# A comparison on GpSimd written with one operation or with two, in a fused attention and feed-forward kernel

## The chip, the cores and the metric

The kernel runs on one core of a Trainium2 chip. A core has five engines that run side by side and meet at semaphores: TensorE (PE, matrix products; its weight loads are shown apart as PEld), VectorE (DVE), ScalarE (ACT), GpSimd (POOL) and SyncE (SP, which here issues transfers). The metric is the device time of one execution in microseconds, as the median of several executions. The kernel before takes 563.74 us (563.67 to 563.99 in 3 runs).

## The reference

Eight batches of eight heads go through attention in which every score that lies more than tau = 0.02 below its row's maximum is dropped. The result, 4608 rows of 512, goes through an RMS norm and a gated feed-forward layer.

```python
scores = scale * np.matmul(q, k.transpose(0, 1, 3, 2))          # 8 x 8 x 576 x 576, head size 64
thresh = np.max(scores, axis=-1, keepdims=True) - tau
scores = np.where(scores >= thresh, scores, -1000000000.0)
attn = np.exp(scores - np.max(scores, axis=-1, keepdims=True))
attn = attn / (np.sum(attn, axis=-1, keepdims=True) + 1e-09)
x = np.matmul(attn, v)                                          # heads side by side: 4608 x 512
xn = x / np.sqrt(np.mean(x * x, axis=-1, keepdims=True) + 1e-06) * rms_g
g = xn @ w_gate                                                 # 512 -> 1536
out = (g * (1.0 / (1.0 + np.exp(-g))) * (xn @ w_val)) @ w_out   # 1536 -> 512
```

The change concerns the third line: the choice of the scores that stay.

## The kernel before

The work is cut into 144 steps. A step is 128 rows of queries and two heads (h = 0 and 1). PE writes the scores of a step to PSUM (`s_ps`). DVE copies them to SBUF (`ssb`), with the sign turned and scaled, and takes the minimum over each row on the way (`mx`), so a high score is a low number there. GpSimd adds tau to it; this is the row's threshold (`nth`):

```python
def ttr(o, h=h):                                   # L592, DVE
    nc.vector.tensor_tensor_reduce(
        out=ssb[a][:, h], in0=s_ps[h][:, ROW_AT:ROW_AT + S], in1=zrow, scale=-1.0 / 8.0, scalar=3.0e38,
        op0=ALU.add, op1=ALU.min, accum_out=mx[m][:, h:h + 1])
...
def nthr(o):                                       # L599, GpSimd
    nc.gpsimd.tensor_scalar(out=nth[m], in0=mx[m], scalar1=tau, scalar2=None, op0=ALU.add)
```

The dropping and the exponential are done in one of two ways for each head of a step. From step 16 on, head 1 of every even step goes the way "g", and all else the way "p":

```python
if way == "p":
    def prelu(o, h=h):                             # L610, ACT: scores below the threshold become hugely negative
        nc.scalar.activation(out=ssb[a][:, h], in_=ssb[a][:, h], func=PRELU, scale=-1.0,
                             bias=nth[m][:, h:h + 1], **PRELU_KW)
    def ex(o, h=h):                                # L614, ACT
        nc.scalar.activation(out=wsb[s % NW][:, h], in_=ssb[a][:, h], func=AF.Exp)
    def ex2(o):                                    # L617, ACT: both heads at once, where both go this way
        nc.scalar.activation(out=wsb[s % NW], in_=ssb[a], func=AF.Exp)
    ...
else:
    def ex(o, h=h, es=es):                         # L629, ACT
        nc.scalar.activation(out=esb[es], in_=ssb[a][:, h], func=AF.Exp, scale=-1.0,
                             bias=nth[m][:, h:h + 1])
    ...
        def mask(o, h=h):                          # L643, GpSimd: 1 where the score stays, else 0
            nc.gpsimd.tensor_scalar(
                out=wsb[s % NW][:, h], in0=ssb[a][:, h], scalar1=nth[m][:, h:h + 1], scalar2=None,
                op0=ALU.is_le)
        def take(o, h=h, es=es):                   # L648, GpSimd: times the exponential
            nc.gpsimd.tensor_tensor(out=wsb[s % NW][:, h], in0=wsb[s % NW][:, h], in1=esb[es],
                                    op=ALU.mult)
```

From step 16 on the weights `wsb` of a step are turned by a transposing DMA (`wt<-wsb`, L677, issued by SyncE). After every odd step PE multiplies the transposed weights of the two steps with V (L696, L700), and DVE divides by the row sums (L717, L718). Four steps make a chunk of 128 rows of x. For each chunk ACT sums squares, and GpSimd normalizes:

```python
def mean(o):                                       # L732, L734, GpSimd
    nc.gpsimd.tensor_scalar(out=irm[i3], in0=ssq[i3], scalar1=1.0 / DM, scalar2=1e-6,
                            op0=ALU.mult, op1=ALU.add)
    nc.gpsimd.tensor_tensor(out=ir[i3], in0=irm[i3], in1=mhalf, op=ALU.pow)
def norm(o):                                       # L737, GpSimd
    nc.gpsimd.tensor_scalar(out=xn[ci % 2], in0=xsb[ci % 2], scalar1=ir[i3], scalar2=1.0,
                            op0=ALU.mult, op1=ALU.mult)
```

GpSimd also rounds V and the weights of the feed-forward layer to float16 (L487, L937), in the same two-operation form. The feed-forward layer (L795, L800, L865 on PE; L809 on ACT; L812, L817 on DVE) runs in between, on chunks that are complete. The instructions of all engines are put into one fixed order before the program is built, by a list scheduler with a table of estimated costs; the estimates set the order only.

Of the kernel before, what the change touches and what calls it, by code (L numbers as in the profile page):

```python
# [11 lines left out]
ALU = mybir.AluOpType  # L12
# [115 lines left out]
def kernel(  # L128
# [26 lines left out]
    def sb(name, shape, dt=FP32):  # L155
        return konst.tile(shape, dt, tag=name, name=name)
# [26 lines left out]
    ssb = [sb(f"ssb{i}", [128, 2, S]) for i in range(NSS)]  # L183
    NES = 3
    mx = [sb(f"mx{i}", [128, 2]) for i in range(6)]
    nth = [sb(f"nth{i}", [128, 2]) for i in range(6)]
    esb = [sb(f"esb{i}", [128, S], FP16) for i in range(NES)]
    NW = 3
    wsb = [sb(f"wsb{i}", [128, 2, S], FP16) for i in range(NW)]
# [31 lines left out]
    def add(eng, cost, prio, deps, fn, **kw):  # L221
        o = Op(eng, cost, prio, deps, fn, **kw)
        ops.append(o)
        return o
# [361 lines left out]
    def emit_softmax(s, so):  # L586

        a = s % NSS
        m = s % 6
        for h in range(2):  # L590
            def ttr(o, h=h):
# [4 lines that stand above are left out]
            ttr_of[s, h] = add("DVE", COST["ttr"], s - 1, [so, o_c] + exp_of.get(s - NSS, []), ttr)  # L596

        def nthr(o):
            nc.gpsimd.tensor_scalar(out=nth[m], in0=mx[m], scalar1=tau, scalar2=None, op0=ALU.add)  # L599

        tn = add("POOL", COST["pool_tiny"], s - 4, [ttr_of[s, 0], ttr_of[s, 1]], nthr)
        wfree = [w_read.get(s - NW)]
        done = []
        ways = WAYS[s % len(WAYS)] if s >= FIRST else "pp"
        pls = []
        for h in range(2):
            way = ways[h]
            if way == "p":
                def prelu(o, h=h):
                    nc.scalar.activation(out=ssb[a][:, h], in_=ssb[a][:, h], func=PRELU, scale=-1.0,  # L610
                                         bias=nth[m][:, h:h + 1], **PRELU_KW)

                def ex(o, h=h):
                    nc.scalar.activation(out=wsb[s % NW][:, h], in_=ssb[a][:, h], func=AF.Exp)  # L614

                def ex2(o):
                    nc.scalar.activation(out=wsb[s % NW], in_=ssb[a], func=AF.Exp)  # L617

                pls.append(add("ACT", COST["prelu"], s + 0.5, [tn], prelu))
                if ways != "pp":  # L620
                    done.append(add("ACT", COST["exp0"], s + 0.5, pls + wfree, ex))
                elif h:
                    done.append(add("ACT", COST["exp2"], s + 0.5, pls + wfree, ex2))
            else:
                es = pre.get("n", 0) % NES
                pre["n"] = pre.get("n", 0) + 1

                def ex(o, h=h, es=es):
                    nc.scalar.activation(out=esb[es], in_=ssb[a][:, h], func=AF.Exp, scale=-1.0,  # L629
                                         bias=nth[m][:, h:h + 1])  # L630

                e = add("ACT", COST["exp1"], s + 0.4, [tn, pre.get(("es", es))], ex)
                if way == "d":
                    def mask(o, h=h, es=es):
                        nc.vector.scalar_tensor_tensor(
                            out=wsb[s % NW][:, h], in0=ssb[a][:, h], scalar=nth[m][:, h:h + 1], in1=esb[es],
                            op0=ALU.is_le, op1=ALU.mult)

                    st = add("DVE", COST["mask_d"], s + 0.4, [e] + wfree, mask)
                    done.append(st)  # L640
                else:
                    def mask(o, h=h):
                        nc.gpsimd.tensor_scalar(  # L643
                            out=wsb[s % NW][:, h], in0=ssb[a][:, h], scalar1=nth[m][:, h:h + 1], scalar2=None,
                            op0=ALU.is_le)

                    def take(o, h=h, es=es):
                        nc.gpsimd.tensor_tensor(out=wsb[s % NW][:, h], in0=wsb[s % NW][:, h], in1=esb[es],  # L648
                                                op=ALU.mult)

                    mk = add("POOL", COST["mask_g"], s + 0.4, [tn] + wfree, mask)
                    st = add("POOL", COST["take_g"], s + 0.4, [e, mk], take)
                    done.append(mk)
                pre["es", es] = st
                done.append(st)
        exp_of[s] = done

        if s < N_PE or s < N_ALT and s % 2:
            def tr(o):
                for j in range(9):  # L660
                    r, c = divmod(j, 5)
                    nc.tensor.transpose(ring[o.slot[r]].bitcast(FP16)[:, 128 * c:128 * c + 128],  # L662
                                        wsb[s % NW].rearrange("p h s -> p (h s)")[:, 128 * j:128 * j + 128], id16)

            t = add("PE", COST["trw"], s + 2.4, done + av_of.get(s - NWT, []), tr, ring="R", nring=2)
            w_read[s] = t
            w_ready[s] = []
            for r, (lo, hi) in enumerate(((0, 5), (5, 9))):
                def ev(o, r=r, lo=lo, hi=hi):
                    eng = nc.gpsimd if W_EVAC[r] == "POOL" else nc.vector  # L670
                    eng.tensor_copy(out=wt[s % NWT][:, lo:hi], in_=ring[t.slot[r]].bitcast(FP16)[
                        :, 0:128 * (hi - lo)].rearrange("p (c n) -> p c n", n=128))

                w_ready[s].append(add(W_EVAC[r], COST["evac_w" if W_EVAC[r] == "DVE" else "evac_wp"], s + 2.4, [t], ev, frees=(t, r)))
        else:
            def tdma(o):
                nc.sync.dma_start_transpose(out=wt[s % NWT], in_=wsb[s % NW].rearrange("p h s -> p (h s)"))  # L677

            t = add("SP", COST["sp_tr"], s, done + av_of.get(s - NWT, []), tdma, dma=DMA_NS['wt'])
            w_read[s] = t  # L680
            w_ready[s] = [t]
# [265 lines left out]
    for j in range(4):  # L947
        o = add("POOL", COST["pool_dma"], W_FROM + W_STEP * n + j + WO_AT, [], lambda o, j=j: nc.gpsimd.dma_start(
            out=wo[:, 3 * j:3 * j + 3], in_=wo_src[:, 3 * j:3 * j + 3]), dma=DMA_NS['wo'], bulk=True)
# [111 lines left out]
```

## Time and profile before

| engine | busy, us | what it mostly does |
|---|---|---|
| PE | 554.2 | scores, products with V, feed-forward layer |
| ACT | 460.0 | exponentials, `prelu`, tanh |
| DVE | 425.3 | copy with minimum, gating, dividing |
| POOL | 322.4 | comparison 110.5, product with the exponential 81.8, thresholds 31.7, normalizing 25.0 |

The span of the profiled execution is 561.9 us, and the granted TensorE clock is full throughout. The times of engines overlap, so they don't add up to the span. In the page, a group of instructions is shown by its line in the kernel, its engine and operation, and what it writes and reads; then comes how often it ran, its busy time, the mean of one in ns, and the idle time of its engine right before it with the engine, tile and line that ended it. An engine that is busy for half the span may still hold up the others, and one that is idle costs nothing if nobody waits for it; so the chain that ended last and the waits are read beside the busy times.

### The profile page before, as it was taken

What the parts mean: (1) busy time and instruction counts of PE and PEld (TensorE: products, weight loads), DVE (VectorE), ACT (ScalarE), POOL (GpSimd) and SP (SyncE); (2) the same over time, 40 slices, a digit from 0 to 9 for tenths busy, and PEclk for the clock granted to TensorE, in tenths of its full rate; (3) what the DMA queues carried; (4) which work ended last, traced back from release to release, by engine and by line L of the source; (5) the groups of instructions that cost most, each with busy time, mean ns of one, the idle gap of its engine ahead of it and who ended that gap; (6) DMA issues with size and microseconds to landing.
All of it is one profiled execution on the core that took longest, in us unless ns stands there. A gap on an engine that the chain in (4) does not pass through costs nothing.

```text
span 561.9 us, 15217 instructions
## 1 busy us (share of the span) xinstructions
PE 554.2 (99%) x5768; PEld 316.4 (56%) x5768; DVE 425.3 (76%) x1091; ACT 460.0 (82%) x741; POOL 322.4 (57%) x462
## 2 busy tenths in 40 slices
PE   8999999999999999999999999999999999999997
PEld 4756666757667455545555455545555444445674
DVE  4989977869968589658885889578966886586354
ACT  5999999998989788879888997888988988885332
POOL 2378846975767456665667666666666664551000
PEclk9999999999999999999999999999999999999999
DMA  9999999889976499889997799989998544652211
GB/s 200 271 291 250 173 179 216 161 143 198 195 181 115 116 174 160 185 156 183 154 176 175 121 170 176 182 177 156 174 189 179 110 97 97 151 95 53 85 38 38
DMA packets 270025, 89.08 MB, mean 159 GB/s; under 512 B 252544, under 2 KB 262272, under 8 KB 269952
## 3 DMA queue, kind: packets, MB, share of 16 engines
q1 hardware_dynamic: 267168, 86.02, 76.4%
q0 software_dynamic: 1600, 1.57, 1.7%
q8 instruction: 45, 0.74, 0.6%
q10 hardware_dynamic: 1184, 0.52, 0.3%
q14 instruction: 28, 0.23, 0.1%
HBM read 37.75 MB, written 9.44 MB: 84 GB/s over the span
## 4 chain that ended last, share of the span: by engine, by line
PE 95%; DVE 2%; POOL 1%; ACT 1%; issue 1%; DVEq 0%; POOLq 0%
PE s_ps L569 29%; PE ring L795 17%; PE ring L800 16%; PE ring L865 15%; PE ring L700 6%; PE ring L304 2%; PE ring L696 2%; DVE ssb L592 1%; PE ring L662 1%; PE ring L365 1%; PE s_ps L800 1%; PE s_ps L840 1%; PE s_ps L865 1%; PE s_ps L262 1%; PE s_ps L795 0%
## 5 line engine op out<-in xcount | busy, mean ns | idle before, releaser
L592 DVE CUSTOM_DVE_ANT_0 ssb<-s_ps,zrow 128x576 f32<-128x576 f32 x288 | 207.1, 753 | 64.3 <-PE s_ps L569 46.5
L610 ACT ACTIVATE ssb<-ssb,nth 128x576 f32<-128x576 f32 x224 | 166.1, 767 | 26.7 <-POOL nth L599 26.2
L569 PE MATMUL s_ps<-qkt 64*64 64x288 f32 (+1 forms) x1792 | 166.4, 417 | 1.5 <-DVE mx L592 1.5
L643 POOL TENSOR_SCALAR wsb<-ssb,nth 128x576 f16<-128x576 f32 x64 | 110.5, 1726 | 11.6 <-DMA wt<-wsb 6.3
L795 PE MATMUL ring<-xnT,wg 128*128 128x256 f16 (+1 forms) x564 | 114.4, 325 | 0.3 <-DVE xsb L718 0.3
L569 PEld LDWEIGHTS s_ps<-qkt 64*64 64x64 f32 (+1 forms) x1792 | 78.4, 140 | 62.8 <-DVE mx L592 15.5
L800 PE MATMUL ring<-xnT,wv 128*128 128x512 f16 (+1 forms) x528 | 110.4, 331 | 0.0
L599 POOL TENSOR_SCALAR nth<-mx 128x2 f32<-128x2 f32 x144 | 31.7, 220 | 128.6 <-DVE mx L592 114.4
L812 DVE SCALAR_TENSOR_TENSOR sl<-th,ring 128x256 f32<-128x256 f32 (+1 forms) x141 | 77.0, 546 | 30.5 <-ACT th L809 29.5
L617 ACT ACTIVATE wsb<-ssb 128x1152 f16<-128x1152 f32 x80 | 93.0, 1162 | 3.4 <-DMA wt<-wsb 1.1
L809 ACT ACTIVATE th<-ring 128x256 f32<-128x256 f32 (+1 forms) x141 | 67.7, 481 | 30.7 <-PE ring L795 26.6
L865 PE MATMUL ring<-wo,hf 128*128 128x512 f16 x384 | 90.0, 380 | 0.0
L648 POOL TENSOR_TENSOR wsb<-wsb,esb 128x576 f16<-128x576 f16 x64 | 81.8, 1279 | 10.1 <-ACT esb L629 5.7
L817 DVE TENSOR_TENSOR hf<-ring,sl 128x512 f16<-128x512 f32 (+1 forms) x132 | 75.0, 568 | 9.3 <-PE ring L800 0.5
L800 PEld LDWEIGHTS <-wv 128*128 128x128 f16 x576 | 52.2, 98 | 44.5 <-issue 14.2
L795 PEld LDWEIGHTS <-wg 128*128 128x128 f16 x576 | 52.0, 98 | 42.2 <-issue 12.2
L865 PEld LDWEIGHTS <-hf 128*128 128x128 f16 x408 | 37.3, 98 | 47.0 <-issue 7.0
L629 ACT ACTIVATE esb<-ssb,nth 128x576 f16<-128x576 f32 x64 | 49.2, 769 | 6.4 <-POOL nth L599 6.0
L700 PE MATMUL ring<-va,wt 128*128 128x65 f16 (+1 forms) x1264 | 52.9, 193 | 0.0
L700 PEld LDWEIGHTS <-wt 128*128 128x128 f16 (+1 forms) x1280 | 48.7, 100 | 3.8 <-issue 0.7
L614 ACT ACTIVATE wsb<-ssb 128x576 f16<-128x576 f32 x64 | 43.6, 681 | 1.6
L696 PE MATMUL ring<-va,wt 128*128 128x130 f16 (+1 forms) x158 | 35.1, 227 | 0.6 <-ACT qTv L473 0.6
(68 smaller groups left out, 444.8 us busy)
## 6 DMA issues: line engine op xcount, KB each, us to landing
vst<-in_v_dram SPq DMA_DIRECT2D x32, 256.0 KB, 3.8
qkn<-in_k_dram SPq DMA_DIRECT2D x31, 256.0 KB, 4.5
out_dram<-osb SPq DMA_DIRECT2D x31, 256.0 KB, 2.8
qkn<-in_q_dram SPq DMA_DIRECT2D x28, 256.0 KB, 4.2
stage<-in_moe_w_gate_dram SPq DMA_DIRECT2D x6, 512.0 KB, 6.1
stage<-in_moe_w_val_dram SPq DMA_DIRECT2D x6, 512.0 KB, 6.2
wt<-wsb SPq DMA_TRANSPOSE x128, 3.2
wo<-in_moe_w_out_dram POOLq DMA_DIRECT2D x4, 384.0 KB, 6.9
```

What stands on the lines that cost most here:

```text
L569: nc.tensor.matmul(s_ps[h][rows, ROW_AT + n * part:ROW_AT + n * part + n], lhs(hs), kT[i][p][h][hs, n * part:n * part + n], start=True, st ...
L592: nc.vector.tensor_tensor_reduce(out=ssb[a][:, h], in0=s_ps[h][:, ROW_AT:ROW_AT + S], in1=zrow, scale=-1.0 / 8.0, scalar=3.0e38, op0=ALU.a ...
L610: nc.scalar.activation(out=ssb[a][:, h], in_=ssb[a][:, h], func=PRELU, scale=-1.0, bias=nth[m][:, h:h + 1], **PRELU_KW)
L617: nc.scalar.activation(out=wsb[s % NW], in_=ssb[a], func=AF.Exp)
L643: nc.gpsimd.tensor_scalar(out=wsb[s % NW][:, h], in0=ssb[a][:, h], scalar1=nth[m][:, h:h + 1], scalar2=None, op0=ALU.is_le)
L648: nc.gpsimd.tensor_tensor(out=wsb[s % NW][:, h], in0=wsb[s % NW][:, h], in1=esb[es], op=ALU.mult)
L700: nc.tensor.matmul(ring[o.slot[0]][rs, at:at + D + 1], w[:, 5 * h + j, rs], va[vi][:, p, 2 * j + h], start=False, stop=(h == 1 and j == 3))
L795: nc.tensor.matmul(ring[o.slot[0]][:, 0:n], wg[d][:, fs], xnT[slot][:, d, 0:n], start=(d == 0), stop=(d == 3))
L800: nc.tensor.matmul(ring[o.slot[0]][:, 0:n], wv[d][:, fs], xnT[slot][:, d, 0:n], start=(d == 0), stop=(d == 3))
L812: nc.vector.scalar_tensor_tensor(out=sl[i][:, 0:n], in0=th[i][:, 0:n], scalar=1.0, in1=ring[g.slot[0]][:, 0:n], op0=ALU.add, op1=ALU.mult)
L817: nc.vector.tensor_tensor(out=hf[hi][:, 0:n], in0=ring[vv.slot[0]][:, 0:n], in1=sl[i][:, 0:n], op=ALU.mult)
L865: nc.tensor.matmul(ring[(first or o).slot[0]], hf[hs[fc][0]][:, 128 * j:128 * (j + 1)], wo[:, fc], start=(fc == 0), stop=(fc == NFC - 1))
```

## The change

The comparison L643 gets a second operation, a multiplication by 1.0. The value stays 0 or 1, so the result is the same. It is meant to give GpSimd the comparison in the form that its other long operations in this kernel have. The order of instructions and the estimates of the scheduler stay as they are.

```diff
                     def mask(o, h=h):
                         nc.gpsimd.tensor_scalar(
-                            out=wsb[s % NW][:, h], in0=ssb[a][:, h], scalar1=nth[m][:, h:h + 1], scalar2=None,
-                            op0=ALU.is_le)
+                            out=wsb[s % NW][:, h], in0=ssb[a][:, h], scalar1=nth[m][:, h:h + 1], scalar2=1.0,
+                            op0=ALU.is_le, op1=ALU.mult)
```

## The prediction

> **What bounds the kernel now.** I read the page from the top: busy shares, then the slices of the span, then the chain that ended last. After that I asked the trace for the busy time by stretches, for the groups of GpSimd by form, and for the waits of PE and of GpSimd.
>
> ```profile
> PE 554.2 (99%) x5768; PEld 316.4 (56%) x5768; DVE 425.3 (76%) x1091; ACT 460.0 (82%) x741; POOL 322.4 (57%) x462
> PE   8999999999999999999999999999999999999997
> POOL 2378846975767456665667666666666664551000
> PE 95%; DVE 2%; POOL 1%; ACT 1%; issue 1%; DVEq 0%; POOLq 0%
> ```
>
> PE is busy in 99% of the span, in every slice, and makes up 95% of the chain that ended last; POOL (GpSimd), the engine that the change touches, is busy 57% and holds 1% of the chain. The changed instruction runs between 59.6 and 503.3 us only. In that stage the busy time by stretches reads:
>
> ```profile
> 60.00:500.00 440.00, 439.09 (x4675) 243.90 (x4673) 342.90 (x875) 383.34 (x613) 281.38 (x381) 1.00 0.84 161
> ```
>
> The columns are the stretch, its length, then busy time of PE, PE's weight loads, DVE, ACT and POOL. PE lacks 440.00 − 439.09 = 0.9 us of being busy throughout. GpSimd is idle for 440.00 − 281.38 = 158.6 us. PE's own list of waits names no DMA and no GpSimd:
>
> ```profile
> PE s_ps L569 <- DVE mx L592: 1.5, 4, 0.4
> PE s_ps L262 <- DVE zrow L257: 1.2, 1, 1.2
> PE ring L696 <- ACT qTv L473: 0.6, 1, 0.6
> ```
>
> So the kernel waits for TensorE's work, and a better GpSimd instruction can at most remove waits that PE hardly has.
>
> [...] So the 99% may hide short stalls; here the weight loads are busy for 56% only. I therefore allow some microseconds more than the visible 0.9. [...] The trace agrees with the reported spans here: a mask starts at 202.62 and its product at 204.43, 1.81 us apart, for a mask of 1.73 us.
>
> [...]
>
> **The change, part by part.** It takes no instruction away and adds none. 64 comparisons (one head of every even step from step 16 on) get a second operation, a multiplication by 1.0. Their output is 0 or 1 as before. Order, semaphores and buffers stay. What can change is the duration of one instruction. The groups of GpSimd by form:
>
> ```profile
> L643 POOL TENSOR_SCALAR wsb<-ssb,nth 128x576 f16<-128x576 f32 x64 | 110.5, 1726 | 11.6 <-DMA wt<-wsb 6.3
> L648 POOL TENSOR_TENSOR wsb<-wsb,esb 128x576 f16<-128x576 f16 x64 | 81.8, 1279 | 10.1 <-ACT esb L629 5.7
> L599 POOL TENSOR_SCALAR nth<-mx 128x2 f32<-128x2 f32 x144 | 31.7, 220 | 128.6 <-DVE mx L592 114.4 <-DVE rz L717 3.1 <-DMA wt<-wsb 2.8
> L737 POOL TENSOR_SCALAR xn<-xsb,ir 128x512 f16<-128x512 f32 x36 | 25.0, 695 | 3.7
> L732 POOL TENSOR_SCALAR irm<-ssq 128x1 f32<-128x1 f32 x36 | 6.9, 190 | 21.9 <-ACT xn L729 19.6
> ```
>
> The comparison (L643) has one operation; it takes 1726 ns for 576 elements a partition. Normalizing x (L737) is the same kind of instruction, float32 in and float16 out, a scalar by the row, but with two operations (multiply, multiply by 1.0): 695 ns for 512. Two lines through these points:
> - two operations: L732 with 1 element 190 ns, L737 with 512 elements 695 ns: (695 − 190) / 511 = 0.99 ns an element.
> - one operation: L599 with 2 elements 220 ns, L643 with 576 elements 1726 ns: (1726 − 220) / 574 = 2.62 ns an element.
>
> The single form is also 30 ns dearer at hardly any elements, and L599 is an addition, not a comparison. This speaks for a better loop behind the two-operation form, not only for a slow comparison. But no row shows one operation of arithmetic on a long tile, nor a comparison with two. Three outcomes for the instruction:
> - **The pair takes the better loop** (my 60%): 190 + 575 × 0.99 = 759 ns, estimated from the rows above[...]. At 759 ns GpSimd saves 64 × (1726 − 759) = 62 us, and its busy time falls from 322 to some 260 us.
> - **The comparison sets the rate** and the multiplication adds little (25%): 1.7 to 2.0 us, GpSimd +0 to +18 us.
> - **The pair falls onto a slower loop** (15%): 3 us or more, GpSimd +80 us or more.
>
> **What of it lies on the path.** GpSimd's stream in one pair of steps:
>
> ```profile
> 202.62 1.73 POOL L643 TENSOR_SCALAR wsb<-ssb,nth 128x576 f16<-128x576 f32 x1
> 204.43 1.28 POOL L648 TENSOR_TENSOR wsb<-wsb,esb 128x576 f16<-128x576 f16 x1
> 205.80 0.19 POOL L732 TENSOR_SCALAR irm<-ssq 128x1 f32<-128x1 f32 x1
> 206.07 0.57 POOL L734 TENSOR_TENSOR ir<-irm,mhalf 128x1 f32<-128x1 f32 x1
> 206.74 0.69 POOL L737 TENSOR_SCALAR xn<-xsb,ir 128x512 f16<-128x512 f32 x1
> 207.52 0.23 POOL L599 TENSOR_SCALAR nth<-mx 128x2 f32<-128x2 f32 x1
> 210.39 0.21 POOL L599 TENSOR_SCALAR nth<-mx 128x2 f32<-128x2 f32 x1 [2.65 <-DVE mx L592]
> 210.71 1.73 POOL L643 TENSOR_SCALAR wsb<-ssb,nth 128x576 f16<-128x576 f32 x1
> ```
>
> The weights of the even step are complete at 204.43 + 1.28 = 205.71; their transposing DMA is issued at 205.74 and, with the page's median of 3.2 us to landing, is there at 208.9. The product with V that needs them (L696) starts on PE at 216.38, together with the odd step's weights, which are issued at 210.44 and there at 213.6. A mask 0.97 us shorter brings the even weights sooner to a consumer that leaves them lying 7.4 us already. The odd step's threshold at 207.52 could come sooner too, as DVE's maximum was ready at about 206.3; but the product with V has 216.38 − 213.6 = 2.8 us to spare there. And right after, GpSimd waits 2.65 us for DVE. So most of the saved 62 us turns into waits for DVE's maximum, which are 114.4 us already. ACT's waits for the threshold, 26.2 us (L610) and 6.0 us (L629), may shrink, but ACT at 82% doesn't bound either.
>
> Contention: the maximum on DVE (L592) takes 746 to 759 ns over all its 288 runs, with the mask beside it or not. [...] I count nothing for it.
>
> The sum with the better loop: −0.9 us at most from visible PE idle time in the stage, of which a part is due to other things, and as much again from hidden stalls: −0.5 us as the middle, −2.5 at best. With the comparison setting the rate: 0 to +0.5 us.
>
> **Rivals.** (1) GpSimd becomes the bound. Against it: 158.6 us idle in the stage over 64 masks is 2.5 us for each, so a mask must grow to about 4.2 us before GpSimd is full. But its stream is in order, and thresholds sit behind masks, so from about 3.5 us PE would wait: at 4.5 us I'd expect (4.5 − 4.2) × 64 = 19 us and some more for waits, 3 to 6% slower. This needs the slower loop, and a bad one. (2) The transposing DMAs are the real gate, and weights that come sooner move them into other loads. For it: the DMA engines are 84% busy in the stage, and one pair of transposes took 3.96 us to issue. Against it: PE names no wait for a DMA. It would make ±1 us. (3) PE's 99% hides stalls that GpSimd causes through the chain threshold, ACT, weights. For it: weight loads waited 17.4 us for DVE's maximum. Against it: those gaps are about 0.4 us, as long as gaps with no releaser, and GpSimd is not named. If a third of it went, the time would be 558 us, still within 2%.
>
> **Range and chances.** 0.60 × (−0.5) + 0.25 × (+0.2) leaves about −0.3; the slow loop is a tail, not the middle. I say 563.2 us. The range from 560.5 to 566.0 us holds the first two outcomes and a mild form of the third. 2% is 11.3 us: faster by that would need stalls that no view shows (2%); slower needs a mask above some 4 us (8%).
>
> **What would show it.** [...] PE's busy time at 552 to 555 us, its waits as before. The step fails if the mask stays near 1.7 us. The conclusion fails if PE's busy time or idle time moves by more than 3 us, or if waits of PE for transposed weights appear.

## The result, and the profile after

The changed kernel takes 568.5 us (568.31 to 568.87 in 4 runs) against 563.87 us before (563.67 to 564.53 in 4 runs): a ratio of 1.0079, with a 95% interval from 1.0065 to 1.0093. It is 4.6 us slower, outside the predicted range of 560.5 to 566.0 us, though within 2%. The order of the instructions is the same on every engine.

First the groups of GpSimd by form, as shown of before (busy us, mean ns, then the idle time in front and what ended it):

```profile
L643 POOL TENSOR_SCALAR wsb<-ssb,nth 128x576 f16<-128x576 f32 x64 | 142.0, 2219 | 8.4 <-DMA wt<-wsb 3.0
L648 POOL TENSOR_TENSOR wsb<-wsb,esb 128x576 f16<-128x576 f16 x64 | 81.8, 1278 | 9.7 <-ACT esb L629 5.2
L599 POOL TENSOR_SCALAR nth<-mx 128x2 f32<-128x2 f32 x144 | 31.9, 221 | 107.6 <-DVE mx L592 86.8 <-DVE rz L717 7.0 <-DMA wt<-wsb 5.1
```

The comparison went from 1726 to 2219 ns. That is 0.49 us more for each of 64, or 31.6 us of GpSimd. Its neighbours didn't move. Then the busy times, and the shares of the chain that ended last:

```profile
PE 557.7 (98%) x5768; PEld 318.3 (56%) x5768; DVE 425.1 (75%) x1091; ACT 458.1 (81%) x741; POOL 354.1 (63%) x462
PE 91%; DVE 3%; ACT 2%; issue 2%; DMA 1%; POOL 1%; SPq 0%; DVEq 0%; ACTq 0%; POOLq 0%
```

GpSimd has 31.7 us more and still idles for more than a third. PE is still shown busy for 98%, with 3.5 us more busy time for the same matmuls; a move of more than 3 us was the prediction's own sign that its conclusion fails. In the list of waits for ACT (us in total, how often, the longest) one line grew from 26.2 us:

```profile
ACT ssb L610 <- POOL nth L599: 41.2, 43, 2.4
```

Where PE lost its time shows when the starts of PE's 5768 weight loads are compared between the two traces. The table gives how much later they start a few us behind a place than a few us ahead of it, where this is 0.25 us or more:

| time before, us | delay added, us | PE's instruction there |
|---|---|---|
| 115.6 | 0.8 | scores, L569 |
| 140.7 | 0.5 | transposes of q and k, L304 |
| 173.6 | 0.5 | product with V, L696 and L700 |
| 218.0, 228.8 | 0.3, 0.4 | scores, L569 |
| 258 to 262 | 0.5 | scores, L569, and transposes, L304 |
| 314.8, 441.0 | 0.3, 0.4 | scores, L569 |

These sum to 3.8 us (from unrounded values). Four smaller steps, at 94.6, 327.4, 385.9 and 402.6 us, add 0.5 us, which makes the 4.3 us by which PE's last weight load is later; the span grew by 4.4 us.

One of the places, the one at 228.8 us, followed backward. The kernel before, in order of time (start, duration, engine, line, what; the bracket is the idle time in front):

```profile
218.16 1.73 POOL L643 TENSOR_SCALAR wsb<-ssb,nth 128x576 f16<-128x576 f32 x1
...
223.05 0.23 POOL L599 TENSOR_SCALAR nth<-mx 128x2 f32<-128x2 f32 x1
223.31 1.44 ACT L610 ACTIVATE ssb<-ssb,nth 128x576 f32<-128x576 f32 x2 [0.83 <-POOL nth L599]
224.78 1.16 ACT L617 ACTIVATE wsb<-ssb 128x1152 f16<-128x1152 f32 x1
225.85 0.58 ACT L809 ACTIVATE th<-ring 128x512 f32<-128x512 f32 x1
226.46 0.69 DVE L812 SCALAR_TENSOR_TENSOR sl<-th,ring 128x512 f32<-128x512 f32 x1 [0.65 <-ACT th L809]
227.07 0.75 DVE L592 CUSTOM_DVE_ANT_0 ssb<-s_ps,zrow 128x576 f32<-128x576 f32 x1
...
227.74 0.75 DVE L592 CUSTOM_DVE_ANT_0 ssb<-s_ps,zrow 128x576 f32<-128x576 f32 x1
...
228.83 1.20 PE L569 MATMUL s_ps<-qkt 64*64 64x288 f32 x16
```

And the changed kernel:

```profile
220.57 2.22 POOL L643 TENSOR_SCALAR wsb<-ssb,nth 128x576 f16<-128x576 f32 x1
...
224.24 0.19 POOL L732 TENSOR_SCALAR irm<-ssq 128x1 f32<-128x1 f32 x1
224.51 0.57 POOL L734 TENSOR_TENSOR ir<-irm,mhalf 128x1 f32<-128x1 f32 x1
225.18 0.69 POOL L737 TENSOR_SCALAR xn<-xsb,ir 128x512 f16<-128x512 f32 x1
225.96 0.23 POOL L599 TENSOR_SCALAR nth<-mx 128x2 f32<-128x2 f32 x1
226.22 1.44 ACT L610 ACTIVATE ssb<-ssb,nth 128x576 f32<-128x576 f32 x2 [1.54 <-POOL nth L599]
227.69 1.16 ACT L617 ACTIVATE wsb<-ssb 128x1152 f16<-128x1152 f32 x1
228.76 0.58 ACT L809 ACTIVATE th<-ring 128x512 f32<-128x512 f32 x1
229.37 0.69 DVE L812 SCALAR_TENSOR_TENSOR sl<-th,ring 128x512 f32<-128x512 f32 x1 [1.35 <-ACT th L809]
229.98 0.75 DVE L592 CUSTOM_DVE_ANT_0 ssb<-s_ps,zrow 128x576 f32<-128x576 f32 x1
...
230.66 0.75 DVE L592 CUSTOM_DVE_ANT_0 ssb<-s_ps,zrow 128x576 f32<-128x576 f32 x1
...
231.07 1.60 PE L569 MATMUL s_ps<-qkt 64*64 64x288 f32 x16
```

From the start of the comparison to the start of the threshold it is 5.39 us instead of 4.89, the 0.5 us that the comparison got longer; what stands between them (L648, L732, L734, L737) is the same. ACT waits 0.7 us longer for the threshold (1.54 against 0.83). Behind `prelu` and the exponential in ACT's fixed order stands a tanh of the feed-forward layer, which has nothing to do with the threshold; behind that tanh, in DVE's order, stand the gating and the next maximum. PE's next scores need the buffers which that maximum empties: their weight loads are shown waiting for it, once for 0.42 us in the kernel before, for 0.42 and 0.21 us in the changed one. DVE's wait grew by the same 0.7 us (1.35 against 0.65), and the 16 matmuls of the scores take 1.60 us instead of 1.20: 4 of them start from 231.07 us on, the other 12 only from 231.47 us on, after the second maximum (230.66 + 0.75 = 231.41). The stall shows as duration of the group, not as idle time of PE; this far PE's 99% could hide stalls, as the prediction allowed.

At 173.6 us the threshold reaches PE by another way, and there PE's list of waits shows it, with 1.1 us where the kernel before had 0.6:

```profile
PE ring L696 <- ACT qTv L473: 1.1, 1, 1.1
```

The copy that ends this wait (L473) stands in ACT's order behind a `prelu` that waits 0.76 us for its threshold in place of 0.26; the kernel before, then the changed one:

```profile
169.67 1.44 ACT L610 ACTIVATE ssb<-ssb,nth 128x576 f32<-128x576 f32 x2 [0.26 <-POOL nth L599]
171.59 1.44 ACT L610 ACTIVATE ssb<-ssb,nth 128x576 f32<-128x576 f32 x2 [0.76 <-POOL nth L599]
```

### The profile page after: what moved, and what is told of

It reads as the page before. It is cut to its first block, busy times and chain, and to the rows that moved or that the text cites. A ratio compares the mean times of both kernels' runs of the same rounds, so it can differ in the third digit from the quotient of the medians.

```text
span 566.3 us, 15217 instructions
## 1 busy us (share of the span) xinstructions
PE 557.7 (98%) x5768; PEld 318.3 (56%) x5768; DVE 425.1 (75%) x1091; ACT 458.1 (81%) x741; POOL 354.1 (63%) x462
## 4 chain that ended last, share of the span: by engine, by line
PE 91%; DVE 3%; ACT 2%; issue 2%; DMA 1%; POOL 1%; SPq 0%; DVEq 0%; ACTq 0%; POOLq 0%
PE s_ps L569 28%; PE ring L795 16%; PE ring L800 16%; PE ring L865 15%; PE ring L700 6%; PE ring L304 2%; PE ring L696 2%; DVE ssb L592 1%; DMA stage<-in_moe_w_gate_dram 1%; PE s_ps L800 1%; PE s_ps L840 1%; PE s_ps L865 1%; PE ring L662 1%; PE ring L365 1%; ACT ssb L610 1%
## 5 line engine op out<-in xcount | busy, mean ns | idle before, releaser
L569 PE MATMUL s_ps<-qkt 64*64 64x288 f32 (+1 forms) x1792 | 168.9, 417 | 1.6 <-DVE mx L592 1.5
L643 POOL TENSOR_SCALAR wsb<-ssb,nth 128x576 f16<-128x576 f32 x64 | 142.0, 2219 | 8.4 <-DMA wt<-wsb 3.0
L569 PEld LDWEIGHTS s_ps<-qkt 64*64 64x64 f32 (+1 forms) x1792 | 80.0, 140 | 63.8 <-DVE mx L592 16.5
L648 POOL TENSOR_TENSOR wsb<-wsb,esb 128x576 f16<-128x576 f16 x64 | 81.8, 1278 | 9.7 <-ACT esb L629 5.2
L700 PE MATMUL ring<-va,wt 128*128 128x65 f16 (+1 forms) x1264 | 52.8, 193 | 0.0
L700 PEld LDWEIGHTS <-wt 128*128 128x128 f16 (+1 forms) x1280 | 48.7, 100 | 4.3 <-issue 1.2
L696 PE MATMUL ring<-va,wt 128*128 128x130 f16 (+1 forms) x158 | 35.1, 227 | 1.1 <-ACT qTv L473 1.1
```

Of the source, the lines that this page charges most:

```text
L569: nc.tensor.matmul(s_ps[h][rows, ROW_AT + n * part:ROW_AT + n * part + n], lhs(hs), kT[i][p][h][hs, n * part:n * part + n], start=True, st ...
L643: nc.gpsimd.tensor_scalar(out=wsb[s % NW][:, h], in0=ssb[a][:, h], scalar1=nth[m][:, h:h + 1], scalar2=1.0, op0=ALU.is_le, op1=ALU.mult)
L700: nc.tensor.matmul(ring[o.slot[0]][rs, at:at + D + 1], w[:, 5 * h + j, rs], va[vi][:, p, 2 * j + h], start=False, stop=(h == 1 and j == 3))
```

## The experiments

All times are medians, and all ratios are to runs of the kernel before on the same chip (563.80 to 564.23 us).

**Forms of the instruction by themselves.** Eighteen forms run on GpSimd after all else.

```diff
+ts(s1, ALU.is_le, None, None); ts(s1, ALU.is_le, 1.0, ALU.mult); ts(s1, ALU.mult, None, None)
+ts(s1, ALU.mult, 1.0, ALU.mult); ts(s1, ALU.mult, 1.0, ALU.add)
+...                     # s1: threshold column; 128 x 576, float32 to float16; each three times
```

> The kernel before, with 18 forms of GpSimd's tensor_scalar on 128 x 576 float32 to float16 (three at 288 elements) run three times each after all else, on tiles that nobody reads any more; its time means nothing, the durations do. If a comparison sets the rate, comparing with one operation takes 1.73 us, with a second operation 2.2 us whichever it is and in whichever place, and one operation of arithmetic is quick (0.76 us or less). If one operation is the slow form, as the prediction took from the threshold's row, multiplying with one operation takes some 1.7 us and multiplying twice 0.75 us.

Durations of the single instructions in the trace, the medians of three repetitions that agree within 10 ns:

| operations (p: column, else a constant) | ns |
|---|---|
| one: is_le p; is_ge p; mult p; add p; max p | 1728; 1735; 1732; 1733; 1728 |
| one with a constant: is_le; mult | 1652; 1653 |
| two with a constant: is_le, mult 1 | 2140 |
| two: is_le p, mult 1; is_le p, add 0; mult 1, is_le p | 2216; 2220; 2220 |
| two: add p, max 0; subtract p, max 0 | 2212; 2212 |
| two: mult p, mult 1; mult p, add 1 | 749; 749 |
| at 288 elements: is_le p; is_le p, mult 1; mult p, mult 1 | 1008; 1256; 507 |

In the timeline of GpSimd the pairs stand out; these lines are two with a constant (is_le alone, then is_le and mult), one of mult then is_le, and one mult alone:

```profile
570.08 3.88 POOL L991 TENSOR_SCALAR wsb<-ssb 128x576 f16<-128x576 f32 x2
574.07 2.22 POOL L991 TENSOR_SCALAR wsb<-ssb,nth 128x576 f16<-128x576 f32 x1
576.37 1.65 POOL L991 TENSOR_SCALAR wsb<-ssb 128x576 f16<-128x576 f32 x1
```

Each expectation holds in part. The comparison with a second operation takes 2.2 us in either place, as the first has it; but the comparison isn't what is slow: each single operation tried with the column takes 1.73 us, a multiplication too, as the second has it. And a second operation isn't what is quick: with the column, a pair that begins with a comparison, an addition or a subtraction, or ends with a comparison, takes 2.21 or 2.22 us. Among the forms tried, only a multiplication followed by a multiplication or an addition runs in 0.75 us.

**A quick instruction in the place of the comparison.** What it leaves out is told in its expectation.

```diff
-scalar1=nth[m][:, h:h + 1], scalar2=None, op0=ALU.is_le)
+scalar1=nth[m][:, h:h + 1], scalar2=1.0, op0=ALU.mult, op1=ALU.add)
```

> The comparison is replaced by two arithmetic operations (score times threshold, plus 1.0), so the output keeps every score of the head that goes this way: the dropping of 64 of 288 score tiles is left out. If two arithmetic operations run in the quicker loop, the instruction takes 0.76 us in place of 1.73 us and GpSimd's busy time falls by 62 us. My theory (PE is full in the kernel before, and only lateness costs) expects 563.9 us, within 0.7 us of the kernel before. The rival (the time follows GpSimd's occupancy in both directions, at the 4.6 us for 31.6 us that the change showed) expects 4.6 x 62 / 31.6 = 9 us less, 555 us.

It took 564.09 us against 564.23 us, a ratio of 0.9997 (0.9991 to 1.0004). The busy line, and the group:

```profile
PE 554.3 (99%) x5768; PEld 316.2 (56%) x5768; DVE 426.1 (76%) x1091; ACT 461.7 (82%) x741; POOL 258.5 (46%) x462
...
L643 POOL TENSOR_SCALAR wsb<-ssb,nth 128x576 f16<-128x576 f32 x64 | 47.7, 746 | 10.8 <-DMA wt<-wsb 4.8 <-ACT ssb L610 0.9
```

64 us less on GpSimd bring nothing that can be measured (at best 0.5 us, by the interval). The time doesn't follow GpSimd's busy time downward. That agrees with the theory that only lateness costs.

**The same length elsewhere.** The comparison of before, and a separate instruction after the product.

```diff
 nc.gpsimd.tensor_tensor(out=wsb[s % NW][:, h], in0=wsb[s % NW][:, h], in1=esb[es], op=ALU.mult)
+nc.gpsimd.tensor_scalar(out=pado[:, 0:272], in0=stage[0][:, 0, 0:272], scalar1=1.0, scalar2=1.0,
+                        op0=ALU.mult, op1=ALU.mult)
```

> The comparison keeps its one operation; a separate GpSimd instruction of about 0.42 us on tiles that nobody reads follows each product with the exponential, so GpSimd's stream gets the same 0.5 us longer, but after the weights of the step are done. If what costs is that thresholds queue behind a longer stream, the time is that of the changed kernel, 567 to 569 us. If what costs is that the weights of the even step are ready later for their transposing DMA, the time stays at 564 to 565 us, as those weights are not delayed by their own pad.

It took 567.23 us, a ratio of 1.0049 (1.0036 to 1.0062). The instruction is 418 ns long. In its trace PE's delay grows at 115.6, 140.7, 173.6, 228.8, 258 to 262, 314.8 and 441.0 us, as in the changed kernel, by 0.2 to 0.7 us. One more step, 1.5 us at 409 us, is a wait for transposed weights that the changed kernel doesn't have. The traced execution took 569.09 us, the longest of six, so that wait may belong to it alone. Most of the loss (3.0 of 4.6 us) needs neither a slow comparison nor even weights that are late by it, only a stream that is half a microsecond longer.

**Both.** The changed kernel with that instruction besides.

> The changed kernel with the separate 0.42 us instruction after each product besides, so GpSimd's stream is 1.0 us longer for each comparison than in the kernel before. If stalls begin once the slack of single places in the stream is used up, each further 0.5 us costs more than the first: 574 to 580 us. If the cost is proportional, 573 us. If it was an accident of the order, about 569 us.

It took 574.23 us, a ratio of 1.0186 (1.0172 to 1.0200), at 379.8 us of GpSimd's busy time. From 258.5 to 322.4 us of GpSimd nothing is lost; the next 31.7 us cost 4.6 us, and 25.7 us beyond that cost another 6 us. A slope that gets steeper was expected of slack that is used up place by place, and the size is at the lower edge of that. But the measured interval (573.5 to 575.1 us) only just leaves out the 573 us of a proportional cost, which itself rests on the 4.6 us with an interval from 3.7 to 5.2. So the steeper slope is not clear of noise.

**Thresholds off GpSimd.** The addition of tau on DVE, with each comparison.

```diff
-nc.gpsimd.tensor_scalar(out=nth[m], in0=mx[m], scalar1=tau, scalar2=None, op0=ALU.add)
+nc.vector.tensor_scalar(out=nth[m], in0=mx[m], scalar1=tau, scalar2=None, op0=ALU.add)
```

> The kernel before, with the threshold's addition of tau on DVE at the same place of the order, so thresholds no longer queue behind GpSimd's long instructions. It is the base for nth_dve_two. DVE gets 144 short instructions of about 0.1 us and their waits; 564 to 572 us by itself.

> As nth_dve_one, with the comparison of two operations (2.22 us instead of 1.73 us). If the loss comes through thresholds that queue behind the comparison, the two kernels agree within 1 us. If it comes through the weights (comparison, product, transposing DMA, product with V) or through GpSimd being full, the second is 4 us slower, as the changed kernel is.

They took 570.94 us (1.0122, 1.0103 to 1.0141) and 572.42 us (1.0137, 1.0124 to 1.0150). The addition takes 0.16 us on DVE, where about 0.1 was expected. The slower comparison costs 1.5 us here in place of 4.6, a little more than the 1 us expected; but the two intervals overlap, and the base is worse by itself. That points to the thresholds and doesn't settle it.

**Thresholds earlier on GpSimd.** The cleaner test: the changed kernel, with the place of the thresholds in GpSimd's stream as the one difference.

```diff
 seq = order_ops(ops, {"R": 4})
+for tn, *tt in nths:                     # the thresholds from step 16 on
+    seq.remove(tn); seq.insert(max(seq.index(x) for x in tt) + 1, tn)
```

> The changed kernel (comparison 2.22 us) with one thing else: from step 16 on, each threshold stands as early in GpSimd's stream as its maximum is planned to be on its way, mostly one instruction earlier (ahead of a normalizing, a rounding or a product). GpSimd's busy time stays at 354 us. If the loss comes through thresholds that queue behind longer work, most of it goes: 564 to 566 us. If it comes through GpSimd's work being too much or through late weights, the time stays at 568 us or more, as the product and the normalizing come later here.

It took 565.91 us, a ratio of 1.0035 (1.0021 to 1.0048) against the changed kernel's 1.0079 (1.0065 to 1.0093): more than half of the loss is gone, with GpSimd as busy as in the changed kernel. The place followed above, in this kernel:

```profile
223.96 0.23 POOL L599 TENSOR_SCALAR nth<-mx 128x2 f32<-128x2 f32 x1
224.26 0.19 POOL L732 TENSOR_SCALAR irm<-ssq 128x1 f32<-128x1 f32 x1
224.29 1.43 ACT L610 ACTIVATE ssb<-ssb,nth 128x576 f32<-128x576 f32 x2
...
227.99 0.69 DVE L812 SCALAR_TENSOR_TENSOR sl<-th,ring 128x512 f32<-128x512 f32 x1 [0.25 <-ACT th L809]
```

ACT no longer waits for the threshold, DVE's wait for the tanh is down from 1.35 to 0.25 us, and PE's delay doesn't grow there. The busy times in the stretch from 100 to 120 us, where the largest stall was (stretch, length, then PE, weight loads, DVE, ACT, POOL), first of the kernel before, then of the changed kernel:

```profile
100.00:120.00 20.00, 20.00 (x264) 13.13 (x262) 17.33 (x51) 18.83 (x34) 16.83 (x23) 1.00 0.85 146
100.00:120.00 20.00, 19.92 (x252) 12.80 (x248) 16.71 (x49) 16.83 (x30) 18.46 (x23) 1.00 0.74 137
```

and of this one:

```profile
100.00:120.00 20.00, 20.00 (x270) 13.20 (x268) 17.59 (x52) 18.28 (x32) 18.68 (x22) 1.00 0.74 143
```

GpSimd is as full as in the changed kernel, above 90%, yet PE's delay grows by 0.1 us in this stretch in place of 0.8. (The counts of matmuls, 264, 252 and 270, also depend on where the stretch cuts PE's stream.) It was not GpSimd's fullness that cost this time, but what stood behind what.

**The same on the kernel before.**

> The kernel before (comparison of one operation) with the thresholds one place earlier in GpSimd's stream, as in thr_first_two. If the kernel before has no stall from late thresholds, 563.5 to 564.5 us, the same as before; if it had some, as the rival of the prediction (hidden stalls) has it, 561 to 563 us.

It took 563.88 us against 563.92 us, a ratio of 0.9998 (0.9990 to 1.0006). With the comparison of 1.73 us no threshold was late enough to cost anything that shows: at best 0.6 us, by the interval. ACT's waits for thresholds before `prelu` fell to 11.8 us here, from 26.2, so their total alone doesn't say what they cost.

**The order planned anew.**

```diff
-mask_d=750.0, mask_g=1740.0, take_g=1300.0, ...
+mask_d=750.0, mask_g=2230.0, take_g=1300.0, ...
```

> The changed kernel with the scheduler's estimate of the comparison raised from 1740 to 2230 ns, so that the order of all engines is planned with the true length. If the loss is a matter of order, 563.5 to 566 us; if of GpSimd's time as such, 568 us.

It took 565.29 us (564.70 to 568.91), a ratio of 1.0034 (1.0020 to 1.0048). An order planned with the true length takes as much of the loss away as the earlier thresholds do.

**What is left.** With earlier thresholds PE's last weight load is 1.8 us later than in the kernel before. Its delay grows by 0.4 us near 70 us, as in the trace of the quick instruction, where most of it is made up again by 120 us; by 0.5 us at 173.6 us, where the threshold still stands behind the product and ACT's wait is 0.76 us as in the changed kernel; and by 0.8 us at 149.8 us, with a wait that neither of the first two kernels has:

```profile
PE ring L304 <- DMA qkn<-in_q_dram: 0.7, 1, 0.7
```

SyncE issues that load of q at 145.90 us; in the kernel before at 144.14. In front of it, one ahead of a load of k and one behind it, stand two transposing DMAs of weights, with 1.39 and 1.90 us on SyncE (1.32 and 2.03 in the kernel before). That they waited for late weights there was my guess. So I let 16 loads pass the transpose ahead of them.

> thr_first_two (comparison of two operations, thresholds one place earlier) with 16 positions of SyncE's stream changed: a load of q or k that stood right behind a transposing DMA stands ahead of it. If what is left of the loss, some 2 us, comes from loads that queue on SyncE behind transposes that wait for late weights, 564 to 565 us, and PE's wait for the q load near 150 us goes. If it comes from something else, it stays at 565.9 us.

It took 574.14 us (570.04 to 575.10), a ratio of 1.0180 (1.0163 to 1.0198), far from both expected times. In the trace, of the execution of 570.04 us, the wait for q went, as expected, but the first line of PE's waits is now a new one:

```profile
PE ring L696 <- DMA wt<-wsb: 4.0, 4, 2.2
```

The product with V waits for transposed weights instead. So the order on SyncE matters both ways. How much of the remaining 2 us comes by it no run settles: the 0.8 us at the load of q is read from one trace.

## Why the prediction was wrong

- **The bound.** That PE is full before and a quicker instruction would bring next to nothing held: with the comparison at 746 ns the time is unchanged (0.9997). The −0.5 us given to that case lies at the edge of the interval. Two of its sums don't come out: 0.9 us and as much again are 1.8 us at best, not 2.5, and 563.74 less 0.3 is 563.4, not 563.2. Neither changes the argument.
- **The instruction.** The step that failed first is "the pair takes the better loop (my 60%)". The two lines through the rows were good: 190 + 575 × 0.99 = 759 ns for the quick form, which measured 749 ns, and one operation with the column is indeed slow, in each of the five kinds tried (1728 to 1735 ns). (Its "loop" was my word for a rate: the runs show ns an element, and not what makes them.) The fault was to read "two operations" as what the quick rows had in common. They were all multiplications followed by a multiplication or, in L732, an addition, and the forms experiment shows that this counts. The second outcome, 1.7 to 2.0 us since "the multiplication adds little", was mis-sized as well: 2.22 us lies between it and the third, of 3 us or more.
- **The path.** The step that would have been wrong in any case, and that the 4.6 us come from, is "0 to +0.5 us" for a slower comparison. It came from an average, 2.5 us of GpSimd idle for each comparison, and from one pair of steps, in which the odd step's weights lie ready 2.8 us before the product with V. At other places the slack is smaller. From 100 to 120 us GpSimd was busy for 16.83 of 20 us before the change. And the threshold has a second way to PE, shorter than the one by the weights: `prelu`, a tanh behind it, the gating behind that, the maximum, the scores. I had read the first part of this chain (GpSimd, ACT's wait of 26.2 us) and dismissed it since "ACT at 82% doesn't bound either". And PE's list, read as naming no GpSimd, did hold one wait that ends with ACT's order behind a threshold, `PE ring L696 <- ACT qTv L473`: the 0.6 us that became 1.1.
- **The rivals.** The first rival named the right thing, "its stream is in order, and thresholds sit behind masks", but put its beginning at 3.5 us a mask; it had begun by 2.22 us. The third, stalls of the kernel before hidden in PE's 99%, is refuted as far as GpSimd causes them: neither a quicker instruction nor earlier thresholds gained. The second, transposing DMAs as the gate, may have some truth in what is left over: the 0.8 us at the load of q behind them, in one trace.
- **Contention.** Nothing counted, and rightly: DVE's maximum took 753 ns before and 752 after.

## What to carry to other kernels

Slack is a property of a place, not of an engine: before lengthening an instruction on an engine that idles a third of the time, look for a short result in its queue (here a threshold of 0.2 us) that other engines' queues wait for, and follow what stands behind it in each of them until the bound engine. When a row of a profile serves as a model for an instruction, match the operations themselves, not only their number, type and shape (here 749 ns for one pair and 2216 ns for another). And where the order was planned with estimates, a changed duration calls for planning it again.

## What the runs showed of the hardware

GpSimd's `tensor_scalar` (float32 to float16, 128 partitions) ran in three speeds in the forms run, here as slopes between 288 and 576 elements, with the column as the first operand: 0.84 ns an element, (749 − 507) / 288, for a multiplication followed by a multiplication (or by an addition, 749 ns at 576 elements too); 2.5 ns, (1728 − 1008) / 288, for a single comparison; 3.3 ns, (2216 − 1256) / 288, for comparing and multiplying. A lone multiplication by the column takes 1732 ns, and with a further multiplication by 1.0 it takes 749 ns: the instruction that does more is the quicker one of these two. Among the forms tried, this holds only where a multiplication or an addition follows a multiplication.
